# First attention block regrouped from head pairs to token tiles, with a 128-token first FFN step

## Chip, cores and metric

The kernel runs on one core of one Trainium2 chip. The metric is device time in microseconds (us): the median of 3 runs of the kernel before is 591.53 us (591.43 to 591.8).

## What is computed

Chunked attention with memory tokens, then a two-matrix feed-forward network (FFN) with a clipped quadratic gate. All inputs and outputs are float32.

```python
B, H, S, D = 4, 8, 768, 64            # 24 chunks of 32 queries in each sequence
for c in range(S // 32):
    q_c = q[:, :, 32*c : 32*c + 32]
    k_full = concat(mem_k, k[:, :, max(0, 32*c - 16) : min(S, 32*c + 32 + 8)])   # 8 + 56 keys
    v_full = concat(mem_v, v[ same rows ])
    out[:, :, chunk] = softmax(q_c @ k_full.T / sqrt(D)) @ v_full
x = out as (3072 tokens, 512)
h = x @ w_in                           # 512 x 2048
g = where(h >= 1, h, where(h <= -1, 0, (h + 1)**2 / 4))
y = g @ w_out                          # 2048 x 512
```

## The kernel before

The 3072 tokens are six blocks of 512 (TB). A block's FFN has 16 steps `fc`, one for each 128 rows of the hidden layer. A step's *hidden* part is 12 matmuls into one PSUM tile `ps_h` (x and w are each split into a high and a low float32r part, and three of the four products are kept, over four slices of the model dimension); ScalarE (ACT) then takes Relu and Square of it, VectorE (DVE) the minimum with the linear branch (*least*), ACT rounds that to `gh`, DVE forms the rest `gl`; the step's *out* part multiplies them by a slice of w_out into one accumulator bank for each 128 tokens (banks of tags `a0`, for tokens 0 to 255 of the block, and `a1`, for the others).

Weights come as 16 packed slices w_0 to w_15, which ACT and DVE must decode before use: a Prelu on ACT, a shift and an or on DVE, a copy that makes the high part on ACT, a subtraction that makes the low part on DVE (`decode`, L160). The first two slices are loaded and decoded in halves, called u0 to u3 here: u0 and u1 are the w_in slices of fc 0 and 1, u2 that of fc 2, u3 the w_out slice of fc 0.

Block 0's attention is done in four groups g0 to g3 (`first_attention`, L238). Before the change a group is 256 tokens and two of the four pairs of heads: g0 and g1 cover tokens 0 to 255, g2 and g3 tokens 256 to 511. Each goes through: scores (PE), maximum and subtraction (DVE), exponential (ACT), sum, reciprocal and multiplication (DVE), four 128x128 transposes (PE), two copies of them into `pt` (ACT), values (PE), a copy that makes the high part `xth` of x (ACT), a subtraction that makes `xtl` (DVE). g0 does its maximum and subtraction in two halves (`HALVED`, L58); g2 takes its exponential and sum in 8 ACT instructions with an accumulator (`SUMMED`, L57). FFN steps of 256 tokens, A (tokens 0 to 255) and B (256 to 511) for fc 0 to 3, follow (`early_step`, L572); J are steps of all 512 tokens. A0 needs g0 and g1; B0 needs g2 and g3.

What the engines do up to the middle of block 1 is one list written by hand or by a planner, `FIRST` (L33): each word advances one chain by one stage, and each engine runs its instructions in the order in which they come out. So an instruction that waits holds up all later ones of its engine. In the list g0 to g3 are the groups, u0 to u3 and w2 to w15 the decodes, A, B, J (and C, D, E for block 1) the FFN steps, n0 to n3 attention of later halves of blocks, and L0 to L39 the loads, in the order of a table (L646): L0 and L1 are the two parts of g0's queries and keys, L2 and L3 those of g1, L8 and L9 of g2, L12 and L13 of g3; L4, L7, L14, L15 the values of g0 to g3; L5, L6, L10, L11 the packed halves u0 to u3; L16 to L29 the slices w2 to w15; L30 the queries and keys of n0. All are issued by SyncE (SP), in order.

`PLACES` (L233) names for each group the pair of PSUM banks of its scores and of its values. From block 2 on the order comes from a regular loop over steps, which the change does not touch.

Of the kernel before, what the change touches and what calls it, by code (L numbers as in the profile page):

```python
# [30 lines left out]


FIRST = """  # L33
    L2 L0 L1 g0 g0 g0 L3 g1 g0 g0 g1 g0 g0 g1 L8 g0 L6 L5 g0 u0 g1 L10 g0 g0 g1 L9 g1 g1 u1 g2 L4 g1
    g1 u1 u0 u0 u2 g0 g2 g0 L12 u0 u0 g2 u2 u1 L13 g3 g2 g1 g0 u1 L7 g2 u2 g2 g0 g3 L11 L16 L14 g3
    L15 L30 g1 u2 g1 L17 g1 g2 g3 L19 A0 g2 A0 g3 g3 g3 u1 u3 g3 A1 A0 L18 g3 w2 g2 g3 u2 g3 u3 u3
    L25 L23 L20 L31 g2 g3 A0 A2 g2 w2 u3 g3 A1 w2 n0 A2 A1 B0 A1 w2 L29 L22 w3 B0 A1 A0 u3 L21 w2 B0
    w3 B0 w5 w3 L28 A2 L27 L26 L24 w3 L32 A0 A1 A3 w5 B1 A3 B0 w5 A3 A2 w3 A2 n0 w5 w4 B1 B1 w4 B0
    B1 B2 A2 B2 B1 B3 B1 B2 J4 B3 n0 n0 w4 w4 B2 A3 n0 w6 B3 w4 A3 B2 n0 J5 w5 A3 B2 B3 w9 J4 w6 J4  # L39
    n0 w6 w9 J4 J6 w6 J4 B3 J5 n0 J5 w7 B3 n0 w6 J7 J5 J4 w7 J6 n0 w8 w7 w7 J5 w7 w8 J6 n0 J5 w8 J8  # L40
    w11 J6 J7 J6 J7 w10 w9 n0 w8 J8 n0 n0 w12 w9 J7 J8 w8 w9 J8 J6 n0 n0 w11 w10 n0 J7 n0 w10 w10
    J10 w11 J9 J9 w11 w13 w10 J8 w12 J9 J10 n1 n1 w11 J7 n1 w12 J10 J9 J12 w12 n1 J10 w12 n1 w14 J10
    n1 J9 w14 n1 w14 J8 J11 J9 J12 w13 J12 n1 w14 J11 J12 J13 J11 C0 w15 J12 J13 J11 w13 n1 n1 n1
    L34 L33 n2 J10 J11 n1 w13 C0 C0 w14 n1 J13 n1 C1 n2 C1 n2 n2 n2 C1 w15 C0 C1 J11 w13 J14 n2 J12
    w15 n2 C1 n2 C0 J13 J14 n1 J14 J14 L36 C2 J13 n1 C2 n1 C2 n2 J15 n2 J13 n1 n2 C3 w15 J14 L35 w15
    C2 J15 J14 n2 n2 J15 J15 C2 n2 n2 C3 D0 C3 J15 D1 D0 n2 n2 D1 C3 J15 n3 D0 J15 D1 n2 C3 n2 D2
    J15 n2 J15 D3 C0 C1 D3 D0 D2 n2 D3 n2 D0 D2 n3 n2 E5 D1 D3 n2 D2 E4 C2 n2 D3 D2 D1 E4 J15 E5 E4
    C3 n3 n3 E4 E6 E5 n3 n3 n3 E4 n3 D0 D1 E8 n3 D2 E5 D3 E6 E5 E6 E6 n3 E8 E4 E7 E6 n3 E8 E8 E7 E8
    n3 E5 E6 E7 E9 E10 L38 L37 E9 E7 E7 E9 E10 E10 n3 E7 E9 E9 n3 E13 E8 n3 E10 E12 E9 E10 E10 E12
    n3 E13 E12 n3 E13 E13 E13 E12 E11 E14 E11 E12 n3 n3 E11 n3 E14 E11 n3 E11 E15 E15 E14 E15 L39  # L50
    E11 n3 E12 E14 E14 n3 E15 n3 E15 E13
"""
# [784 lines left out]
```

## Time and profile before

| | |
|---|---|
| median of 3 runs | 591.53 us |
| the profiled execution's own time | 591.96 us |
| its span | 590.1 us |
| PE (matmul) busy | 574.4 us, 97% |
| PEld (weight load) busy | 474.8 us, 80% |
| DVE busy | 332.2 us, 56% |
| ACT busy | 267.7 us, 45% |
| chain that ended last, by engine | PE 85%, DVE 6%, ACT 5%, DMA 1% |

Times in the trace are microseconds from the start of the span. Busy shares are means over stages with different limits, so the stages have to be read one by one. A row of the timeline gives start, duration, engine, line (all are L72, the helper that records every instruction), operation, output <- input, count, and in brackets the idle time before it and what ended it. Rows that merge several instructions give their joint duration; matmuls overlap, so the distance from one start to the next is the pace.

### The profile page before, as it was taken

How to read it: one execution, taken by the hardware profiler on the slowest of the kernel's cores; microseconds unless marked ns; L12 is line 12 of the kernel's file. 1: busy time of each engine (PE TensorE's matmuls, PEld its weight loads, DVE VectorE, ACT ScalarE, POOL GpSimd, SP SyncE). 2: the span in 40 equal slices, each digit the busy share in tenths (PEclk: the TensorE clock that was granted, in tenths of full speed). 3: DMA queues.
4: the chain of work that ended last, by engine and by line, in shares of the span. 5: the costliest groups of instructions: out<-in, count | busy, mean ns of one | idle time of the engine just before them, and what ended most of it. 6: DMA issues, size and time to landing. Idle time of an engine off the chain costs nothing.

```text
span 590.1 us, 12043 instructions
## 1 busy us (share of the span) xinstructions
PE 574.4 (97%) x5364; PEld 474.8 (80%) x5364; DVE 332.2 (56%) x489; ACT 267.7 (45%) x468; POOL 2.4 (0%) x7
## 2 busy tenths in 40 slices
...
GB/s 323 423 419 422 170 147 51 99 67 57 195 0 73 2 0 179 34 41 109 72 1 73 108 72 109 73 1 60 120 72 3 1 1 0 72 0 2 0 1 71
DMA packets 10709, 54.91 MB, mean 93 GB/s; under 512 B 1185, under 2 KB 1185, under 8 KB 6305
## 3 DMA queue, kind: packets, MB, share of 16 engines
...
q8 instruction: 42, 0.69, 0.5%
...
## 4 chain that ended last, share of the span: by engine, by line
PE 85%; DVE 6%; ACT 5%; DMA 1%; issue 1%; SPq 0%; DVEq 0%; ACTq 0%
PE ps_o L72 41%; PE ps_h L72 40%; PE ps_x L72 2%; PE ps_s L72 2%; ACT pr L72 2%; DMA w<-in_first_w_dram 1%; DVE pt L72 1%; DVE f L72 1%; ACT gw L72 1%; ACT f L72 1%; DVE mx L72 1%; DVE gw L72 1%; DVE gl L72 1%; DVE wr L72 1%; ACT w L72 1%
## 5 line engine op out<-in xcount | busy, mean ns | idle before, releaser
L72 PE MATMUL ps_h<-xth,wr 128*128 128x512 f32 (+1 forms) x832 | 195.4, 376 | 1.2 <-ACT pt L72 0.6
L72 PE MATMUL ps_o<-wr,gh 128*128 128x512 f32 x768 | 194.5, 390 | 0.0
L72 PEld LDWEIGHTS ps_h<-xth,wr 128*128 128x128 f32 x832 | 147.5, 188 | 31.6 <-DVE wr L72 0.9
L72 PEld LDWEIGHTS ps_o<-wr,gh 128*128 128x128 f32 x768 | 143.5, 188 | 29.6
L72 DVE SCALAR_TENSOR_TENSOR gw<-ps_h,gw 128x512 f32<-128x512 f32 (+1 forms) x104 | 67.4, 648 | 141.1 <-ACT gw L72 140.4
L72 ACT ACTIVATE gw<-ps_h 128x512 f32<-128x512 f32 (+1 forms) x104 | 58.6, 564 | 178.1 <-PE ps_h L72 173.1
L72 PE MATMUL ps_o<-wr,gl 128*128 128x512 f32 x384 | 106.9, 389 | 0.0
L72 PE MATMUL ps_h<-xtl,wr 128*128 128x512 f32 (+1 forms) x416 | 104.5, 373 | 0.0
L72 DVE TENSOR_TENSOR gl<-gw,gh 128x512 fp32r<-128x512 f32 (+1 forms) x104 | 66.8, 647 | 54.4 <-ACT gh L72 53.8
L72 ACT CAST gh<-gw 128x512 fp32r<-128x512 f32 (+1 forms) x104 | 60.6, 587 | 65.6 <-DVE gw L72 55.6
L72 PEld LDWEIGHTS ps_h<-xtl,wr 128*128 128x128 f32 x416 | 75.0, 188 | 13.9
L72 PEld LDWEIGHTS ps_o<-wr,gl 128*128 128x128 f32 x384 | 72.1, 188 | 15.0
L72 ACT ACTIVATE gw<-gw 128x512 f32<-128x512 f32 (+1 forms) x104 | 62.3, 599 | 3.3
L72 DVE STREAM_TRANSPOSE pt<-pr 32x512 f32<-32x512 f32 (+1 forms) x60 | 41.4, 699 | 1.2
L72 DVE STREAM_TRANSPOSE xt<-xr 32x512 f32<-32x512 f32 (+1 forms) x48 | 33.1, 700 | 6.6 <-ACT xr L72 6.0
L72 ACT ACTIVATE pr<-pr 128x1024 f32<-128x1024 f32 (+1 forms) x12 | 11.4, 952 | 33.2 <-DVE pr L72 33.2
...
L72 DVE COPY ob<-ps_o 128x512 f32<-128x512 f32 (+1 forms) x16 | 9.6, 622 | 23.4 <-PE ps_o L72 23.3
L72 DVE SCALAR_TENSOR_TENSOR f<-w,f 128x1024 uint32<-128x1024 uint32 (+1 forms) x18 | 19.5, 1090 | 3.6 <-ACT f L72 3.4
L72 DVE TENSOR_TENSOR wr<-f,wr 128x1024 fp32r<-128x1024 f32 (+1 forms) x18 | 19.5, 1095 | 1.0 <-ACT wr L72 1.0
L72 ACT CAST wr<-f 128x1024 fp32r<-128x1024 f32 (+1 forms) x18 | 17.0, 951 | 5.9 <-DVE f L72 5.8
...
## 6 DMA issues: line engine op xcount, KB each, us to landing
...
qk<-in_first_qk_dram SPq DMA_DIRECT2D x8, 336.0 KB, 5.9
w<-in_first_w_dram SPq DMA_DIRECT2D x4, 512.0 KB, 8.5
v<-in_first_v_dram SPq DMA_DIRECT2D x4, 512.0 KB, 10.2
```

What stands on the lines that cost most here:

```text
L72: return self.tc.keep_in_program_order(getattr(self.engine, name)(*args, **kwargs))
```

## The change

The groups g0 to g3 become tiles of 128 tokens with all four pairs of heads; g0 is tokens 0 to 127, and so on. The count and size of a group's instructions stay (32 score matmuls, a 512-column softmax, 4 transposes, 16 value matmuls, 512 columns of x); the packed queries, keys and values are laid out anew on the host, with the same bytes in each transfer. One memset of the mask falls away: tile g0 alone holds the first chunk of the sequence. The step A0 is replaced by P0 (tokens 0 to 127) and Q0 (128 to 255), each with 12 hidden matmuls of 128 columns in place of A0's 12 of 256, its own two ACT and DVE passes over 128 columns and 3 out matmuls; they share A0's gate tiles and accumulator banks. P0 needs g0 alone, Q0 g1 alone. A1 to A3 and B0 to B3 stay. The scores go to bank pair s (g1: a0), all values to a1. `FIRST` is another list from beginning to end, the loads included.

```diff
 FIRST = """
-    L2 L0 L1 g0 g0 g0 L3 g1 g0 g0 g1 g0 g0 g1 L8 g0 L6 L5 g0 u0 g1 L10 g0 g0 g1 L9 g1 g1 u1 g2 L4 g1
-    g1 u1 u0 u0 u2 g0 g2 g0 L12 u0 u0 g2 u2 u1 L13 g3 g2 g1 g0 u1 L7 g2 u2 g2 g0 g3 L11 L16 L14 g3
-    L15 L30 g1 u2 g1 L17 g1 g2 g3 L19 A0 g2 A0 g3 g3 g3 u1 u3 g3 A1 A0 L18 g3 w2 g2 g3 u2 g3 u3 u3
-    L25 L23 L20 L31 g2 g3 A0 A2 g2 w2 u3 g3 A1 w2 n0 A2 A1 B0 A1 w2 L29 L22 w3 B0 A1 A0 u3 L21 w2 B0
...
+    L0 L1 L2 L3 g0 g0 g0 L6 u1 g0 g0 g1 g0 L5 L8 L4 L9 L10 g1 g1 g1 g0 g0 u0 u0 g1 g0 g0 u0 g1 g0 g1
+    g2 g1 u1 g1 L13 L12 g2 g0 u0 g0 L11 L7 u2 u0 g2 u2 g3 u1 u2 g0 g2 g0 P0 L16 L14 g1 g1 g3 L30 g2
+    u1 g3 g2 P0 u3 g2 L15 g1 g3 u2 P0 u1 u3 u3 u2 g1 P0 g3 g2 g3 A1 w2 A1 u3 g2 g2 Q0 Q0 g3 w2 g3 A1
+    g3 g3 L19 L17 L18 u3 g2 n0 w2 Q0 P0 A1 g3 Q0 A1 n0 A2 g3 w2 Q0 A2 g3 w2 A2 n0 B0 Q0 P0 L20 L21
+    A3 B0 w3 A2 n0 L23 B0 A3 B1 w4 A1 w3 A3 w3 A2 w4 B1 B1 B0 w3 L25 L31 L29 L22 L27 B2 L26 L24 L28
...
-    PLACES = (("s", "s"), ("a0", "a0"), ("a1", "a1"), ("a1", "s"))
+    PLACES = (("s", "a1"), ("a0", "a1"), ("s", "a1"), ("s", "a1"))
...
-        for r in range(2):
-            for c in range(NCH // 2):
-                t, j = divmod(c, P // CHUNK)
+        for r in range(NP):
+            for j in range(P // CHUNK):
                 for h in range(2):
...
-        hi, lo = (x[:, 2 * u : 2 * u + 2, half * HT : (half + 1) * HT] for x in x_of(0))
+        ps = ps.rearrange("p r (t q) -> p r t q", t=2)
+        hi, lo = (x[:, :, g * P : (g + 1) * P].rearrange("p (r t) q -> p r t q", t=2) for x in x_of(0))
...
-            pair, n = divmod(len(halves), 2)
+            name = f"{blk}{tokens[0] // 2}{fc}"
+            if name not in halves:
+                halves.append(name)
+            pair, n = divmod(halves.index(name), 2)
             key = ("g", pair)
-            halves.append(name)
...
-        tiles = both[key]
-        g, gh, gl = (x[:, n * HT : n * HT + size] for x in tiles)
+        tiles, c0 = both[key], n * HT + (tokens[0] % 2) * P
+        g, gh, gl = (x[:, c0 : c0 + size] for x in tiles)
...
+    parts |= {"P": (0, (0,)), "Q": (0, (1,))}
...
-    k0 = kw[: 2 * (NCH // 2)].reshape(2, NCH // 4, 2, NP, 2, W, D)
+    k0 = kw[: 2 * (NCH // 2)].reshape(NT, 2, 2, NP, 2, W, D)
...
-    v0 = vw[0].reshape(2, 2, 4, NP // 2, 2, 2, W, D).copy()
+    v0 = vw[0].reshape(NT, 4, NP // 2, 2, 2, W, D).copy()
```

With the new list the first instructions of the engines are, in their order (a group's stages by the names used above):

```
PE:  g0 scores, g1 scores, g0 transposes, g2 scores, g1 transposes, g0 values, g3 scores, P0 hidden,
     g1 values, g2 transposes, A1 hidden, g2 values, Q0 hidden, g3 transposes, n0 scores, g3 values,
     A2 hidden, B0 hidden, Q0 out, P0 out, A3 hidden, ...
ACT: u1 Prelu, g0 exp, g1 exp, u0 Prelu, g0 pt, u0 high, u2 Prelu, g2 exps, g0 xth, g1 pt, u1 high,
     P0 Relu and Square, u3 Prelu, g1 xth, g3 exp, u2 high, P0 gh, g2 pt, w2 Prelu, A1 Relu and Square,
     u3 high, g2 xth, Q0 Relu and Square, g3 pt, ...
DVE: g0 max and subtraction (two halves), g1 max, g1 subtraction, g0 sum, u0 shift, g1 sum,
     g0 reciprocal, g0 multiplication, u0 or, g1 reciprocal, g1 multiplication, u1 shift, g2 max, ...
```

Before, they are:

```
PE:  g0 scores, g1 scores, g0 transposes, g2 scores, g1 transposes, g0 values, g3 scores, g1 values,
     g2 transposes, A0 hidden, A1 hidden, g3 transposes, g2 values, g3 values, A2 hidden, n0 scores,
     B0 hidden, A0 out, A1 out, A3 hidden, ...
ACT: g0 exp, u0 Prelu, g1 exp, u1 Prelu, u2 Prelu, g0 pt, u0 high, g2 exps, g1 pt, g0 xth, u1 high,
     u2 high, g1 xth, g3 exp, g2 pt, A0 Relu and Square, u3 Prelu, w2 Prelu, g3 pt, ...
```

## Rows read from the trace of the kernel before

**Rows 1.** The page's first part: span, then busy time, share of the span and number of instructions of each engine.

```profile
span 590.1 us, 12043 instructions
PE 574.4 (97%) x5364; PEld 474.8 (80%) x5364; DVE 332.2 (56%) x489; ACT 267.7 (45%) x468; POOL 2.4 (0%) x7
```

**Rows 2.** Busy time by stage of the span; columns: stage and its length, busy time of PE, PEld, DVE, ACT, POOL (with instructions), granted clock, DMA share, GB/s.

```profile
4.70:12.40 7.70, 2.53 (x128) 1.82 (x129) 4.68 (x12) 1.80 (x4) 0.00 (x0) 1.00 1.01 367
12.40:21.60 9.20, 7.49 (x203) 6.07 (x204) 7.88 (x18) 7.88 (x27) 0.00 (x0) 1.00 1.03 420
21.60:31.00 9.40, 8.42 (x128) 7.28 (x134) 8.20 (x16) 8.09 (x16) 0.00 (x0) 1.00 1.02 425
...
36.00:76.00 40.00, 40.00 (x318) 33.70 (x317) 37.59 (x53) 32.87 (x50) 0.00 (x0) 1.00 0.74 306
76.00:135.00 59.00, 58.43 (x771) 49.12 (x770) 46.19 (x66) 40.79 (x90) 0.00 (x0) 1.00 0.25 91
```

**Rows 3.** Who PE waited for from 40 us to the end: total, times, longest, in us.

```profile
PE ps_h L72 <- DVE gw L72: 0.4, 1, 0.4
PE ps_x L72 <- ACT pr L72: 0.2, 1, 0.2
```

**Rows 4.** Timeline of PE, 4 to 36 us.

```profile
4.68 0.68 PE L72 MATMUL ps_s<-qk 64*32 64x64 f32 x32 [1.61 <-DMA qk<-in_first_qk_dram]
6.56 1.18 PE L72 MATMUL ps_s<-qk 64*32 64x64 f32 x64 [1.19 <-DMA qk<-in_first_qk_dram]
7.89 0.68 PE L72 MATMUL ps_s<-qk 64*32 64x64 f32 x32 [0.15 <-DMA qk<-in_first_qk_dram]
12.41 1.08 PE L72 MATMUL ps_h<-ident,pr 128*128 128x128 f32 x4 [3.84 <-DVE pr L72]
...
21.25 0.66 PE L72 MATMUL ps_h<-ident,pr 128*128 128x128 f32 x4
21.66 0.48 PE L72 MATMUL ps_h<-xth,wr 128*128 128x256 f32 x2
...
28.12 1.15 PE L72 MATMUL ps_x<-pt,v 128*64 128x64 f32 x32 [0.18 <-ACT pt L72]
29.20 1.22 PE L72 MATMUL ps_h<-xth,wr 128*128 128x256 f32 x8
...
30.83 1.48 PE L72 MATMUL ps_s<-qk 64*32 64x64 f32 x128
32.24 1.22 PE L72 MATMUL ps_h<-xth,wr 128*128 128x256 f32 x8
...
33.78 1.09 PE L72 MATMUL ps_o<-wr,gh 128*128 128x512 f32 x4
...
36.53 1.12 PE L72 MATMUL ps_h<-xth,wr 128*128 128x256 f32 x8
...
37.96 1.23 PE L72 MATMUL ps_h<-xth,wr 128*128 128x256 f32 x8
```

**Rows 5.** SP's issues (start, duration; the first five are L2, L0, L1, L3, L8, the next three L6, L5, L10), and then, from one short window for each, the time from issue to landing (last number, us) of L2, L8, L6 and L5.

```profile
0.73 2.27 SPq L72 DMA_DIRECT2D qk<-in_first_qk_dram  x5
3.05 1.60 SPq L72 DMA_DIRECT2D w<-in_first_w_dram  x3
...
qk<-in_first_qk_dram SPq DMA_DIRECT2D x1, 336.0 KB, 3.1
...
qk<-in_first_qk_dram SPq DMA_DIRECT2D x1, 336.0 KB, 6.1
w<-in_first_w_dram SPq DMA_DIRECT2D x1, 512.0 KB, 6.9
w<-in_first_w_dram SPq DMA_DIRECT2D x1, 512.0 KB, 7.7
```

**Rows 6.** Timeline of DVE: g0's mask, g0's last subtraction, g0's multiplication by the reciprocal.

```profile
7.38 0.11 DVE L72 MEMSET ps_s<- 32x64 f32 x1 [6.26 <-PE ps_s L72]
...
8.78 0.42 DVE L72 TENSOR_TENSOR pr<-ps_s,mx 128x256 f32<-128x256 f32 x1
...
11.58 0.69 DVE L72 TENSOR_TENSOR pr<-pr,rin 128x512 f32<-128x512 f32 x1
```

**Rows 7.** ACT: the stretch from g0's copy of `pt` to the end of g3's (length, busy time), then from its timeline the first of g2's exponentials, g1's `pt`, g0's `xth`, two high parts, Relu and Square of A0, two Prelus (u3, and w2 of twice the width), g3's `pt`.

```profile
13.85:28.07 14.22, 12.55 (x35) 1.00 1.02 423
...
16.59 0.31 ACT L72 ACTIVATE pr<-ps_s,mx 128x64 f32<-128x64 f32 x1 [0.25 <-DVE mx L72]
...
18.92 1.19 ACT L72 COPY pt<-ps_h 64x512 f32<-64x512 f32 x2
20.14 0.59 ACT L72 CAST xth<-ps_x 128x512 fp32r<-128x512 f32 x1
20.62 1.14 ACT L72 CAST wr<-f 128x512 fp32r<-128x512 f32 x2
...
24.53 0.38 ACT L72 ACTIVATE gw<-ps_h 128x256 f32<-128x256 f32 x1
24.95 0.42 ACT L72 ACTIVATE gw<-gw 128x256 f32<-128x256 f32 x1
25.27 1.73 ACT L72 ACTIVATE w<-w 128x512 f32<-128x512 f32 x2
26.90 1.17 ACT L72 COPY pt<-ps_h 64x512 f32<-64x512 f32 x2
```

More of the change, by code (lines that the diff above doesn't have):

```diff
@@ L33 @@
 FIRST = """
-    L2 L0 L1 g0 g0 g0 L3 g1 g0 g0 g1 g0 g0 g1 L8 g0 L6 L5 g0 u0 g1 L10 g0 g0 g1 L9 g1 g1 u1 g2 L4 g1
-    g1 u1 u0 u0 u2 g0 g2 g0 L12 u0 u0 g2 u2 u1 L13 g3 g2 g1 g0 u1 L7 g2 u2 g2 g0 g3 L11 L16 L14 g3
-    L15 L30 g1 u2 g1 L17 g1 g2 g3 L19 A0 g2 A0 g3 g3 g3 u1 u3 g3 A1 A0 L18 g3 w2 g2 g3 u2 g3 u3 u3
-    L25 L23 L20 L31 g2 g3 A0 A2 g2 w2 u3 g3 A1 w2 n0 A2 A1 B0 A1 w2 L29 L22 w3 B0 A1 A0 u3 L21 w2 B0
-    w3 B0 w5 w3 L28 A2 L27 L26 L24 w3 L32 A0 A1 A3 w5 B1 A3 B0 w5 A3 A2 w3 A2 n0 w5 w4 B1 B1 w4 B0
@@ L39 @@
[L39 to L48, printed above, removed]
@@ L49 @@
-    n3 E5 E6 E7 E9 E10 L38 L37 E9 E7 E7 E9 E10 E10 n3 E7 E9 E9 n3 E13 E8 n3 E10 E12 E9 E10 E10 E12
-    n3 E13 E12 n3 E13 E13 E13 E12 E11 E14 E11 E12 n3 n3 E11 n3 E14 E11 n3 E11 E15 E15 E14 E15 L39
-    E11 n3 E12 E14 E14 n3 E15 n3 E15 E13
+    L0 L1 L2 L3 g0 g0 g0 L6 u1 g0 g0 g1 g0 L5 L8 L4 L9 L10 g1 g1 g1 g0 g0 u0 u0 g1 g0 g0 u0 g1 g0 g1
+    g2 g1 u1 g1 L13 L12 g2 g0 u0 g0 L11 L7 u2 u0 g2 u2 g3 u1 u2 g0 g2 g0 P0 L16 L14 g1 g1 g3 L30 g2
+    u1 g3 g2 P0 u3 g2 L15 g1 g3 u2 P0 u1 u3 u3 u2 g1 P0 g3 g2 g3 A1 w2 A1 u3 g2 g2 Q0 Q0 g3 w2 g3 A1
@@ new lines @@
+    g3 g3 L19 L17 L18 u3 g2 n0 w2 Q0 P0 A1 g3 Q0 A1 n0 A2 g3 w2 Q0 A2 g3 w2 A2 n0 B0 Q0 P0 L20 L21
+    A3 B0 w3 A2 n0 L23 B0 A3 B1 w4 A1 w3 A3 w3 A2 w4 B1 B1 B0 w3 L25 L31 L29 L22 L27 B2 L26 L24 L28
+    B1 B3 w4 B0 w3 L32 A3 B2 B0 B1 B2 w5 w5 B2 w4 B3 A3 n0 B3 w5 w6 w9 n0 w4 w7 w6 w6 B2 A2 J4 n0 B3
+    w6 J4 n0 B1 J4 w5 B3 w5 J5 w9 J4 J5 B2 A3 n0 B3 n0 J6 n0 w6 w7 J5 J4 w7 n0 n0 J5 J4 J7 n0 J5 n0
+    w8 J6 w7 J7 J6 w11 J6 n0 w7 J7 w9 n0 w8 J6 w10 w14 J8 w8 J5 n0 w8 J8 w9 w8 J8 J8 J8 w9 w10 n1 n1
@@ new lines @@
+    J9 w10 w12 w13 J7 J9 w12 n1 J7 J9 n1 w12 J6 L33 L34 J7 J9 w10 C0 w12 n1 n1 n1 J8 w10 C0 C0 n1 C1
+    J10 w11 n1 w12 J9 w11 w15 C0 C1 w11 w14 C1 n1 n1 w11 n1 J9 C1 J10 C1 n1 J11 n2 w13 C0 J10 w13
+    J11 J11 J10 w13 J11 J13 n1 J10 n2 J13 n2 J10 n2 n2 J12 n2 w14 w14 n2 J11 n2 n1 J11 J12 w13 J13
+    n1 w15 J12 n1 J12 w15 J12 J14 C2 n2 J13 n2 J12 n2 J14 J13 n1 J14 L35 w14 J13 C3 C2 w15 C2 J15 n2
+    w15 n2 C3 J14 n2 n2 C3 J14 n2 C2 J15 J14 D0 n2 L36 J15 n2 J15 J15 D1 C3 n3 D1 n2 D1 J15 n2 J15
@@ L52 @@
+    n2 J15 D0 D0 D0 D1 C0 D2 C2 n2 n2 C3 J15 D2 J15 D0 E5 D1 E5 D2 C1 E4 D0 n2 n3 E5 D1 D2 D3 E5 D3
+    E5 D3 D3 C2 E4 n2 C3 E6 E4 D3 E4 D2 E4 D2 n3 D3 E9 E9 n3 E6 E9 n3 E6 E4 E9 E6 E7 E8 E6 E7 E9 E8
+    E8 E7 E5 n3 n3 E7 E7 E6 E10 n3 L37 E7 n3 E11 n3 E10 E8 n3 E8 E11 E8 E10 E11 n3 E10 E12 E13 n3
+    E10 E11 E12 E12 E14 n3 n3 E9 E10 E12 E12 E11 n3 E13 E13 E14 E11 n3 E15 E12 E13 E13 E14 n3 E15 n3
+    n3 E15 E14 E13 n3 n3 E15 E15 L39 L38 n3 n3 E14
 """
@@ L239, in first_attention @@
         half, u = divmod(g, 2)
-        c0 = half * NCH // 2
-        src = qk_of[0, g].rearrange("p (r n) -> p r n", r=2)
+        src = qk_of[0, g].rearrange("p (r n) -> p r n", r=NP)
         ps = two_banks(PLACES[g][0], "ps_s")[:, :, 0:HT]
-        s = ps.rearrange("p h (r t w) -> p h r t w", r=2, w=W)
-        for r in range(2):
-            for c in range(NCH // 2):
-                t, j = divmod(c, P // CHUNK)
+        s = ps.rearrange("p h (r w) -> p h r w", w=W)
+        for r in range(NP):
+            for j in range(P // CHUNK):
                 for h in range(2):
-                    rows, k0 = slice(h * D, (h + 1) * D), HT + c // 2 * PAIR + c % 2 * (PAIR - W)
+                    rows, k0 = slice(h * D, (h + 1) * D), P + j // 2 * PAIR + j % 2 * (PAIR - W)
                     pe.matmul(
-                        s[j * CHUNK : (j + 1) * CHUNK, h, r, t],
-                        src[rows, r, c * CHUNK : (c + 1) * CHUNK],
+                        s[j * CHUNK : (j + 1) * CHUNK, h, r],
+                        src[rows, r, j * CHUNK : (j + 1) * CHUNK],
                         src[rows, r, k0 : k0 + W],
@@ L256, in first_attention @@
         yield
-        for c in range(NCH // 2):
-            t, j = divmod(c, P // CHUNK)
-            mask(c0 + c, s[j * CHUNK : (j + 1) * CHUNK, :, :, t], c % 2 * NM)
+        for j in range(P // CHUNK):
+            mask(g * P // CHUNK + j, s[j * CHUNK : (j + 1) * CHUNK], j % 2 * NM)
         if u == 0:
@@ L606, in early_step @@
             acc.setdefault(blk, [None] * NT)
-            pair = two_banks(f"a{tokens[0] // 2}", "ps_o")
-            for t in tokens:
-                acc[blk][t] = pair[:, t % 2]
+            if acc[blk][tokens[0]] is None:
+                pair, t = two_banks(f"a{tokens[0] // 2}", "ps_o"), tokens[0] // 2 * 2
+                acc[blk][t : t + 2] = pair[:, 0], pair[:, 1]
         wh, wl = weights(1, fc, 0), weights(1, fc, 1)
@@ L775, in _lay_out @@
     kw = windows(mem_k, k)
-    k0 = kw[: 2 * (NCH // 2)].reshape(2, NCH // 4, 2, NP, 2, W, D)
+    k0 = kw[: 2 * (NCH // 2)].reshape(NT, 2, 2, NP, 2, W, D)
     k0 = _np.concatenate([k0[:, :, 0], k0[:, :, 1, :, :, W // 2 :], k0[:, :, 1, :, :, :NM]], axis=4)
-    k0 = k0.transpose(0, 3, 5, 2, 1, 4).reshape(2, 2 * D, NP, -1)
+    k0 = k0.transpose(0, 3, 5, 2, 1, 4).reshape(NT, 2 * D, NP, -1)
+    q0 = qt[0:2].reshape(2, 2 * D, NP, 2, 128).transpose(0, 3, 1, 2, 4).reshape(NT, 2 * D, NP, 128)
     kw = kw.reshape(NB * 2, NCH // 4, 2, NP, 2, 2, W // 2, D)
```

6 lines of the change are left out of this document (3 added, 3 removed).

## Prediction

> **What bounds the kernel now.** I read the busy shares first: PE is busy for 574.4 of 590.1 us [rows 1], and the chain of waits ends on PE, so time can be won or lost only where PE stands idle, or by more PE work. The table by stage then shows where: 5.17 us idle of the 7.70 from 4.7 us on, 1.71 in the next 9.20, 0.98 in the next 9.40, nothing from 36 to 76, 0.57 in the 59 us after that [rows 2]; from 40 us on PE waits for 0.6 us in all [rows 3]. The regular loop is untouched. So the question is when PE has done one set of work: all of g0 to g3, the scores of n0, the hidden parts of A0, A1, A2 and B0. Before, that is at 33.78 us, where the first out part starts [rows 4]; the set left is the same afterwards (P0 and Q0 with three out matmuls each stand for A0's six).
>
> What holds PE in that stretch? From 12.4 to 31 us DVE is busy for 16.1 and ACT for 16.0 of 18.6 us [rows 2], and PE's waits end on them. So the two queues are near full, and both run strictly in the listed order. I therefore walk the new lists, with start-to-start distances from the rows.
>
> **The start.** Landings in the old order, as issue plus latency or as the PE start that waited: L2 3.83, L0 4.68, L1 6.56, L3 7.89, L8 8.65, L6 9.95, L5 11.25 [rows 4, 5]. They follow the order of issue, so I take landing as a function of kilobytes ahead (336 for queries and keys, 512 for half a slice). In the new order L0 lands at 3.83, L1 at 4.68, L2 and L3 as the second and third pair did, 6.56 and 7.89; L6 is now fifth (1856 KB, between 1680 at 8.65 and 2192 at 9.95) at about 9.1, L5 (2368 KB) at 10.4. g0's scores end about 1.85 us earlier, at 5.4, and its last subtraction at 7.35 instead of 9.2 [rows 6].
>
> This gain is lost at once, in three places. On ACT u1's Prelu is listed ahead of g0's exponential and waits for L6: 9.1 to 9.75, so the exponential ends at 10.3. On DVE g1's maximum and subtraction stand ahead of g0's sum; they need L3 and end at 10.05; the sum runs from 10.35 to 11.05. Then u0's shift stands between g0's sum and its reciprocal: it needs u0's Prelu, which follows g1's exponential, 10.75 to 11.4; the shift ends at 11.85, g1's sum at 12.45, and g0's multiplication runs from 12.6 to 13.3, against 11.58 to 12.27 [rows 6]. The transposes start at 13.45 instead of 12.41 and take 1.08 [rows 4], so g0's `pt` copy starts at 14.5, not 13.85.
>
> **From there ACT sets the pace.** Prices [rows 7]: a pair of `pt` copies 1.18; `xth` 0.52 (0.48 to the next start, 0.59 by itself); a high part 0.57; g2's exponentials 2.33 (16.59 to 18.92); Relu and Square at 256 columns 0.74; a Prelu 0.58, at twice the width 1.05. Check on the old list, from g0's `pt` to g3's: 4 pt, 3 high parts, g2's exponentials, 2 xth, g3's exponential (0.57), A0, u3 and w2 make 12.7, where the row has 12.55 busy of 14.22.
>
> The new list has in the same stretch four high parts (2.28), three xth (1.56), u2's Prelu as well (0.58 more), A1 (0.74) in place of A0, and P0 and Q0. A 128-column Relu and Square is not in the trace; its bounds are half of 0.74 and 0.74. I take 0.53, as two instructions with a fixed part each, so 1.06, and 0.2 for P0's `gh`. The sum: 4.72 + 2.28 + 2.33 + 1.56 + 0.57 + 2.21 + 0.74 + 1.06 + 0.2 = 15.7 us. From 14.5 on, without a wait, g3's `pt` ends at 30.2. Waits: for P0's hidden part about 0.3 (u1's high part ends at 21.6, P0's hidden part at 21.8, after the scores of g3, which need the bank of g2's exponentials), for g2's maximum 0.15, for Q0's hidden part 0.3; I take 0.7 (bounds 0 and the old stretch's 1.67). So 30.9 instead of 28.07.
>
> Ahead of g3's values PE now also has n0's scores, which outlast the copy by 0.2 (1.41 against 1.18); their load L30 comes ahead of L15 on SP now, but at 420 GB/s [rows 2] both are in by about 27. What is left is g3's values 1.08, A2 1.43 (36.53 to 37.96) and B0 1.54 (32.24 to 33.78) [rows 4]: 30.9 + 0.25 + 1.08 + 1.43 + 1.54 = 35.2, against 33.78. **Loss: 1.4 us.**
>
> **The narrow hidden parts.** P0 and Q0 have 24 matmuls of 128 columns where A0 had 12 of 256, at 0.119 us each (1.43 for 12). No float32r matmul of 128 columns is in the trace. From below: half of it, 0.06. The nearest row is the four transposes, also 128 columns against 128x128 weights of 4-byte values: 21.25 to 21.66, 0.103 each. From above: full float32 values, 32 instructions of 64 columns in 1.15 (28.12), 0.072 for each matmul's pair of instructions, 0.144 at twice the columns, and 0.29 if the two heads run side by side. I take 0.119, that is 1.43 for each of P0 and Q0, and the walk has it in it. In the middle of the upper bounds, 0.216, each would be 1.16 longer; P0 and Q0 both stand ahead of ACT instructions that wait for them, so 2.3 us come on top.
>
> On this the Trainium skill speaks too: "TensorE: Matmul & The Clock Gate", section "Back-to-back issue gap", gives some 81 ns a matmul at 128 columns in a sustained stream. The transposes' 103 ns disagree upwards, though they are few; by 81 ns the two parts would be 0.9 shorter in all and the loss about 0.5. Its section "LDWEIGHTS (loading the stationary operand)" has the load of 128 columns at 128/1.2 = 107 ns whatever the rows, which would be the limit at 128 columns; the 103 ns bear that out better, and the loss by it is 1.1.
>
> **Other edits.** One memset less: 0.11 on DVE, before g1's maximum, which waits for L3 anyway. P0's and Q0's extra DVE passes (4 for 2) add some 0.3 us while DVE is 94% busy, 36 to 76 us [rows 2]; PE is then 1.4 later, so its deadlines are too, and this costs nothing; were the cover gone, 0.3. The placement in a1 orders the values behind the previous group's `xtl`, which is earlier on ACT's path already. SP has w5 ahead of w3, so w3 lands 2.5 us later; by its place in the list its low part is due at 44.7 (A2's out part) and ready at about 43.9, so nothing, at worst 1. The later list I could only compare by the same deadlines; the 0.57 us idle after 76 us may go or double.
>
> **Rivals.**
> *Narrow matmuls at 0.216 us.* For it: plain float32 is slow at 64 columns. Against it: the transposes. 1.4 + 2.3 = 3.7 us slower, 595.2. Chance 0.24.
> *The late start is made up.* If `g0` ends its multiplication by 12.3 (landings a microsecond earlier, which needs the gap of 1.88 us between the landings of L0 and L1 [rows 4], where 0.85 is usual, not to come again) the 1.0 goes, and 0.4 is left or nothing. 591.6. For it: the gap may belong to the old pattern; against it: u1's Prelu and u0's shift still stand in the way. Chance 0.17.
> *Faster: P0 and Q0 fill PE's gaps.* PE's idle 2.69 us from 12.4 to 31 closes, less 1.43 of extra PE work: 1.3 us faster, 590.2. Place: PE's queue at P0, which is ready after one group. It decides where g3's `pt` ends before 28: ACT's 15.7 us must then start by 12.3, with g0's multiplication done at 11. For it: g0's scores are 1.85 us earlier; against it: rows 5 for L6 and L5. Chance 0.10.
>
> **How the numbers follow.** The forecast has the chance 0.49. The profiled execution took 591.96, 0.43 over the median; I add the loss to the median: 591.53 + 1.4 = 592.9. Its own range, from no waits on ACT to the 1.67 of old and 0.3 on DVE, is 591.9 to 594.2. Changes under 0.2% (1.18 us) can't be told from none in this kernel. Of the forecast's 0.49, 0.21 lies under that bound; with the late start made up that is 0.38 for no change. Slower: 0.28 + 0.24 = 0.52. Faster: 0.10. The range leaves out half of the faster and a good third of the narrow case: 590.7 to 595.5.
>
> **What would show it.** In the profile after: g0's exponential on ACT behind a Prelu that waited for the load, ending near 10.3; g0's transposes at 13.4; g3's `pt` ending near 31; the first out part on PE at about 35.2; P0's 12 matmuls in 1.4 us (2.6 says the rival). The forecast is wrong if the transposes start before 12.5, if the first out part comes before 34, or if PE has more than 1 us of idle after 36.

## The result and the profile after

The changed kernel took 596.52 us (median of 4, 595.03 to 596.89) against 591.66 us, a ratio of 1.0077 with a 95% interval of 1.0062 to 1.0092: slower by 4.9 us where 1.4 were forecast, and above the range. Five more executions of the same kernel in a later study took 594.13 us (593.56 to 594.42), 1.0043 (1.0030 to 1.0055). Both belong to the answer (the second lies inside the range), and the profiles of one of each show why they differ.

The page of the first profile, its first part, beside [rows 1]:

```profile
span 595.1 us, 12067 instructions
PE 578.7 (97%) x5376; PEld 478.5 (80%) x5376; DVE 332.6 (56%) x490; ACT 267.7 (45%) x471; POOL 2.4 (0%) x7
```

The added work is small: 12 matmuls, 1 instruction on DVE, 3 on ACT. PE's busy time has grown by 4.3 us, though, three times what 12 matmuls at 0.119 us make. By stage (columns as in [rows 2]):

```profile
12.40:21.60 9.20, 7.14 (x172) 5.99 (x173) 7.52 (x19) 6.86 (x24) 0.00 (x0) 1.00 1.04 422
21.60:31.00 9.40, 8.39 (x97) 7.70 (x96) 6.91 (x15) 6.68 (x15) 0.00 (x0) 1.00 1.01 417
...
76.00:135.00 59.00, 58.02 (x762) 48.47 (x762) 47.73 (x66) 43.09 (x91) 0.00 (x0) 1.00 0.20 73
```

From 21.6 to 31 us PE is as busy as before (8.39 against 8.42), but with 97 matmuls instead of 128, and ACT and DVE are busy for 6.7 and 6.9 us instead of 8.1 and 8.2. That suggests that PE is slow and that they wait for it; the timelines show it. PE's timeline, answering to [rows 4]:

```profile
13.47 1.09 PE L72 MATMUL ps_h<-ident,pr 128*128 128x128 f32 x4 [4.86 <-DVE pr L72]
...
16.64 1.98 PE L72 MATMUL ps_x<-pt,v 128*64 128x64 f32 x32
19.61 1.19 PE L72 MATMUL ps_s<-qk 64*32 64x64 f32 x64 [0.99 <-ACT pr L72]
20.72 1.97 PE L72 MATMUL ps_h<-xth,wr 128*128 128x128 f32 x8
22.49 1.05 PE L72 MATMUL ps_h<-xtl,wr 128*128 128x128 f32 x4
23.48 1.98 PE L72 MATMUL ps_x<-pt,v 128*64 128x64 f32 x32
...
29.18 1.15 PE L72 MATMUL ps_x<-pt,v 128*64 128x64 f32 x32
30.26 1.11 PE L72 MATMUL ps_h<-xth,wr 128*128 128x128 f32 x8
31.21 0.61 PE L72 MATMUL ps_h<-xtl,wr 128*128 128x128 f32 x4
...
37.68 0.63 PE L72 MATMUL ps_o<-wr,gh 128*128 128x512 f32 x2
```

P0's hidden part runs from 20.72 to 23.48, 2.76 us; Q0's, the same instructions, from 30.26 to 31.66, 1.40. The 32 value matmuls take 1.98 us at 16.64 and 23.48 and 1.15 at 29.18. Narrow matmuls are not slow; PE ran at about half its pace until some 26 us. On ACT:

```profile
9.20 0.66 ACT L72 ACTIVATE w<-w 128x512 f32<-128x512 f32 x1 [7.18 <-DMA w<-in_first_w_dram]
9.75 1.14 ACT L72 ACTIVATE pr<-pr 128x512 f32<-128x512 f32 x2
...
23.58 0.28 ACT L72 ACTIVATE gw<-ps_h 128x128 f32<-128x128 f32 x1 [1.86 <-PE ps_h L72]
...
24.11 0.67 ACT L72 ACTIVATE w<-w 128x512 f32<-128x512 f32 x1
25.50 0.59 ACT L72 CAST xth<-ps_x 128x512 fp32r<-128x512 f32 x1 [0.73 <-PE ps_x L72]
...
31.86 0.28 ACT L72 ACTIVATE gw<-ps_h 128x128 f32<-128x128 f32 x1 [0.43 <-PE ps_h L72]
...
32.38 1.16 ACT L72 COPY pt<-ps_h 64x512 f32<-64x512 f32 x2
```

ACT stood 1.86 us for P0's hidden part, with g3's chain behind it in its queue, then 0.73 for g1's values (`xth`) and 0.43 for Q0's hidden part: g3's `pt` ends at 33.54, not 30.9, and the first out part starts at 37.68.

### The profile page after: what moved, and what is told of

The parts are those of the page before. It is cut to its first block, busy times and chain, and to the rows that moved or that the text cites. A ratio compares the mean times of both kernels' runs of the same rounds, so it can differ in the third digit from the quotient of the medians.

```text
span 595.1 us, 12067 instructions
## 1 busy us (share of the span) xinstructions
PE 578.7 (97%) x5376; PEld 478.5 (80%) x5376; DVE 332.6 (56%) x490; ACT 267.7 (45%) x471; POOL 2.4 (0%) x7
## 4 chain that ended last, share of the span: by engine, by line
PE 84%; DVE 3%; ACT 3%; issue 1%; DVEq 0%; ACTq 0%
PE ps_o L72 40%; PE ps_h L72 40%; PE ps_x L72 2%; PE ps_s L72 2%; DVE f L72 1%; ACT gw L72 1%; ACT pr L72 1%; DVE gl L72 1%; DVE pt L72 1%; DVE wr L72 1%; ACT wr L72 0%; ACT w L72 0%; ACT gh L72 0%; ACT xth L72 0%; DVE gw L72 0%
## 5 line engine op out<-in xcount | busy, mean ns | idle before, releaser
L72 PE MATMUL ps_h<-xth,wr 128*128 128x512 f32 (+2 forms) x840 | 196.3, 376 | 0.0
L72 PEld LDWEIGHTS ps_h<-xth,wr 128*128 128x128 f32 x840 | 149.6, 190 | 29.0 <-issue 0.2
L72 DVE SCALAR_TENSOR_TENSOR gw<-ps_h,gw 128x512 f32<-128x512 f32 (+2 forms) x105 | 67.4, 643 | 145.7 <-ACT gw L72 145.3
L72 ACT ACTIVATE gw<-ps_h 128x512 f32<-128x512 f32 (+2 forms) x105 | 58.7, 559 | 183.6 <-PE ps_h L72 179.5
L72 PE MATMUL ps_h<-xtl,wr 128*128 128x512 f32 (+2 forms) x420 | 105.6, 374 | 1.0 <-DVE xtl L72 1.0
L72 DVE TENSOR_TENSOR gl<-gw,gh 128x512 fp32r<-128x512 f32 (+2 forms) x105 | 67.3, 644 | 57.9 <-ACT gh L72 57.5
L72 ACT CAST gh<-gw 128x512 fp32r<-128x512 f32 (+2 forms) x105 | 60.5, 581 | 66.2 <-DVE gw L72 52.2
L72 ACT ACTIVATE gw<-gw 128x512 f32<-128x512 f32 (+2 forms) x105 | 62.5, 595 | 3.4
L72 ACT ACTIVATE w<-w 128x1024 f32<-128x1024 f32 (+1 forms) x18 | 18.2, 1035 | 7.2 <-DMA w<-in_first_w_dram 7.2
```

The source lines that it names most:

```text
L72: return self.tc.keep_in_program_order(getattr(self.engine, name)(*args, **kwargs))
```

## The experiments

Times are medians over five rounds; the kernel before ran on the same chip in each study (591.66 to 591.8 us). Theory 1 in the expectations is that PE's slower pace at P0 is the loss, theory 2 that narrow matmuls are slow by themselves, theory 3 that the order of the queues is.

### One group: is it PE's pace, the narrow matmuls or the queues?

**a_warm.** Ten matmuls on zeros into PE's idle time ahead of g0's transposes.

```diff
-    L0 L1 L2 L3 g0 g0 g0 L6 u1 g0 g0 g1 g0 L5
+    L0 L1 L2 L3 g0 g0 g0 L6 u1 g0 g0 g1 K10 g0 L5
...
+    def start_warm(n):
+        keep_warm(n)
+        yield
```

> The changed kernel with ten 512-column bf16 matmuls on zeros put between g1's scores and g0's transposes, into PE's idle time there (8.6 to 13.5 us); nothing of the result depends on them. Theory 1 (PE runs at half pace from 13.5 to 26 us because it had stood idle): P0's 12 hidden matmuls take about 1.45 us instead of 2.76, g1's values 1.15 instead of 1.98, g3's pt copy ends at about 31 instead of 33.5, first out part at about 35.3 instead of 37.7, and the time falls by about 2.3 us. Theory 2 (128-column float32r matmuls are slow there by themselves): P0 stays at 2.7 us and the time within 0.7 us. Theory 3 (only the order of the queues counts, a late start that ACT carries on): no change either, or worse by what the ten matmuls delay the transposes.

596.8 us: no gain. Its PE timeline:

```profile
8.62 4.45 PE L72 MATMUL ps_h<-warm 128*128 128x512 bf16 x10
13.53 0.63 PE L72 MATMUL ps_h<-ident,pr 128*128 128x128 f32 x4 [0.47 <-DVE pr L72]
...
15.89 1.15 PE L72 MATMUL ps_x<-pt,v 128*64 128x64 f32 x32
19.41 0.86 PE L72 MATMUL ps_s<-qk 64*32 64x64 f32 x64 [2.37 <-ACT pr L72]
20.20 1.94 PE L72 MATMUL ps_h<-xth,wr 128*128 128x128 f32 x8
...
38.08 0.50 PE L72 MATMUL ps_o<-wr,gh 128*128 128x512 f32 x1 [0.58 <-issue]
```

After the ten matmuls the pace is up: transposes 0.63 us instead of 1.09, values 1.15. But after the next idle time of 2.4 us, g3's scores still take 0.86 us and P0 then runs at half pace again. Here the granted clock tells it (columns: stage, length, PE busy, granted clock, DMA share, GB/s):

```profile
22.00:24.00 2.00, 2.00 (x25) 0.50 1.00 422
```

So theory 1's remedy failed before it reached P0, and the run decides nothing on its price.

**b_warm.** Eight such matmuls in the kernel before.

```diff
-    L2 L0 L1 g0 g0 g0 L3 g1 g0
+    L2 L0 L1 g0 g0 g0 L3 g1 K8 g0
```

> The kernel before with eight such matmuls between g1's scores and g0's transposes (idle 8.6 to 12.4 us). Theory 1: g0's and g1's transposes (1.1 us each), g2's scores (1.4) and g0's values (1.85) run at full pace, together about 2 us of PE work less, but ACT sets the pace there, so the time falls by 0 to 0.6 us. Theory 3: no change.

591.59 us, ratio 0.9996 (0.9987 to 1.0004).

```profile
20.08 1.98 PE L72 MATMUL ps_x<-pt,v 128*64 128x64 f32 x32
...
33.78 1.09 PE L72 MATMUL ps_o<-wr,gh 128*128 128x512 f32 x4
```

On ACT, first in this run and then, just behind the same place, in the profiled execution of before:

```profile
22.11 0.59 ACT L72 CAST xth<-ps_x 128x512 fp32r<-128x512 f32 x1 [0.43 <-PE ps_x L72]
```

```profile
22.80 0.63 ACT L72 ACTIVATE pr<-pr 128x512 f32<-128x512 f32 x1 [0.56 <-DVE pr L72]
```

Eight such matmuls did not raise the pace: the transposes after them take 1.08 us, and at 20 us PE is at half pace (g1's values 1.98; in the profiled execution of before they took 1.15, at 20.16). And yet the first out part starts at 33.78, as before. ACT waits 0.43 us for the slow values, but in before it waits 0.56 for DVE just behind that place; g3's exponential starts at 22.72 against 22.80. So the kernel before, in these two profiles, does not feel PE's pace up to 22 us: no FFN part stands that early in ACT's queue, and the slower values fall into a wait that is there anyhow.

**a_warm2.** a_warm, and seven more into the free bank pair a0 ahead of g3's scores.

```diff
-    L11 L7 u2 u0 g2 u2 g3 u1
+    L11 L7 u2 u0 g2 H7 u2 g3 u1
...
+    def hold_warm(n):
+        ps = two_banks("a0", "ps_k")[:, 0]
+        for _ in range(n):
+            pe.matmul(ps, warm[:, 0:P], warm, start=True, stop=True)
+        yield
```

> The changed kernel with ten idle matmuls on zeros ahead of g0's transposes and seven more (into the free bank pair a0) ahead of g3's scores, where PE waits for g2's exponentials. In a_warm PE ran at full pace from 13.5 us, but the gap of 2.4 us before g3's scores was followed by half pace again. Theory 1 (PE's pace at P0 is the loss): full pace from 13.5 us on, P0's 12 matmuls in 1.45 us, first out part at about 35.2 us and the time 2 to 2.5 us under the changed kernel's 596.5. Theory 2 (narrow matmuls are slow by themselves, or the pace is not set by the idle time before): P0 still 2.7 us. Theory 3 (queue order alone): P0 faster, but the first out part stays near 37.

595.68 us (594.76 to 598.13). The profiled execution is the slowest of the six:

```profile
17.33 1.68 PE L72 MATMUL ps_k<-warm 128*128 128x512 bf16 x7
...
20.69 1.11 PE L72 MATMUL ps_h<-xth,wr 128*128 128x128 f32 x8
21.64 0.61 PE L72 MATMUL ps_h<-xtl,wr 128*128 128x128 f32 x4
...
36.82 0.50 PE L72 MATMUL ps_h<-xth,wr 128*128 128x256 f32 x2 [1.83 <-issue]
```

Now P0 takes 1.49 us to the next start (20.69 to 22.18): theory 2 falls. The first out part starts at 37.63, though, near 37 as theory 3 has it. Between the two lies a stop of 1.83 us at which PE waits for nothing that the profile knows. Without it the first out part would start at 35.8, where theory 1 has 35.2 and the transposes start 0.6 later than in the changed kernel (14.04 against 13.47). In this execution the granted clock then falls as well, to its lower level for part of two stretches, and 8 matmuls of 256 columns take 1.91 us at 39.63 instead of 1.12:

```profile
38.00:40.00 2.00, 2.00 (x8) 0.57 0.99 414
40.00:42.00 2.00, 2.00 (x13) 0.57 1.06 430
```

(columns: stage, length, PE busy, granted clock, DMA share, GB/s). The other five executions, at 594.8 to 596.5, are no faster than the changed kernel in a_again; they have no profile.

**a_again.** The changed kernel, unaltered.

> The changed kernel once more, for its scatter. Theory 1 (PE's pace at P0 is a matter of when the chip raises it, and P0 stands in ACT's queue, so the time shows it): the times fall into two groups about 2 us apart, near 595 and near 596.8, while those of the kernel before stay together; if the profiled execution is one of the lower group, its P0 takes about 1.45 us and its first out part starts at about 35.3. Rival (one slow pace always, the scatter is something else): P0 takes 2.7 us whatever the time.

594.13 us, and the profiled execution (594.42) is a fast-paced one:

```profile
13.71 1.09 PE L72 MATMUL ps_h<-ident,pr 128*128 128x128 f32 x4 [4.83 <-DVE pr L72]
...
20.64 1.11 PE L72 MATMUL ps_h<-xth,wr 128*128 128x128 f32 x8
...
22.13 1.15 PE L72 MATMUL ps_x<-pt,v 128*64 128x64 f32 x32
...
35.49 0.63 PE L72 MATMUL ps_o<-wr,gh 128*128 128x512 f32 x2
```

```profile
22.23 0.28 ACT L72 ACTIVATE gw<-ps_h 128x128 f32<-128x128 f32 x1 [0.27 <-PE ps_h L72]
...
29.67 0.28 ACT L72 ACTIVATE gw<-ps_h 128x128 f32<-128x128 f32 x1 [0.42 <-PE ps_h L72]
...
30.20 1.16 ACT L72 COPY pt<-ps_h 64x512 f32<-64x512 f32 x2
```

One kernel, two paces: P0 takes 1.49 us (20.64 to 22.13) or 2.76, ACT's wait is 0.27 or 1.86, g3's `pt` ends at 31.36 or 33.54, the first out part starts at 35.49 or 37.68, the span is 592.6 or 595.1. This settles the larger part: 2.2 of the 3.5 us by which the forecast was short are PE's pace at P0 and g1's values. The five new times did not fall into two groups, as expected, but all into the lower one; taken with the first four, this kernel's nine times lie at 593.56 to 595.03 (six) or 596.24 to 596.89 (three). Both groups turn up within one study on one chip in a_start and a_tail below, so it isn't a matter of the chip alone.

### The start, the step, the later list

**a_start.** u1's Prelu behind g0's exponential, u0's Prelu and shift behind g0's multiplication.

```diff
-    L0 L1 L2 L3 g0 g0 g0 L6 u1 g0 g0 g1 g0 L5 L8 L4 L9 L10 g1 g1 g1 g0 g0 u0 u0 g1 g0 g0 u0 g1 g0 g1
+    L0 L1 L2 L3 g0 g0 g0 L6 g0 g0 g1 g0 u1 L5 L8 L4 L9 L10 g1 g1 g1 g0 g0 g1 g0 g0 u0 u0 u0 g1 g0 g1
```

> The changed kernel with the start of the list alone reordered: u1's Prelu behind g0's exponential on ACT, u0's Prelu and shift behind g0's multiplication. All theories: g0's transposes at about 12.3 us instead of 13.47. Theory 3: the 1.1 us are carried on by ACT to the first out part, and the time falls by about 1 us. Theory 1: less, if PE is still slow until 26 us: P0's hidden part stays at 2.7 us, and the time falls by 0.5 to 1 us.

594.94 us, from 593.24 to 596.97: three executions at 593.2 to 594.1, three at 595.8 to 597.0, so its median says little. The profiled one, of the faster three, has P0 at full pace:

```profile
12.61 1.08 PE L72 MATMUL ps_h<-ident,pr 128*128 128x128 f32 x4 [3.89 <-DVE pr L72]
...
34.88 0.63 PE L72 MATMUL ps_o<-wr,gh 128*128 128x512 f32 x2
```

The transposes come 1.10 earlier than in a_again, the first out part only 0.61; the start is carried on, but not whole. The faster executions of the two kernels differ by less (593.2 to 594.1 against 593.6 to 594.4).

**a_A0.** A0 in Q0's place in the list, P0's words dropped.

```diff
-    g3 g3 L19 L17 L18 u3 g2 n0 w2 Q0 P0 A1 g3 Q0 A1 n0 A2 g3 w2 Q0 A2 g3 w2 A2 n0 B0 Q0 P0 L20 L21
+    g3 g3 L19 L17 L18 u3 g2 n0 w2 A0 A1 g3 A0 A1 n0 A2 g3 w2 A0 A2 g3 w2 A2 n0 B0 A0 L20 L21
```

> The changed kernel with A0 (256 tokens) in Q0's place and no P0: what the 128-token step itself costs. Theory 1: P0's 2.76 us at half pace and ACT's wait of 1.86 us for it go, so g3's pt copy ends near 31.3 and the time falls by about 2 us. Theory 3: P0 and Q0 fill time that PE had idle, the time stays within 0.5 us or rises.

595.85 us, neither theory's number: 0.7 under the first median, 1.7 over a_again's. The scatter is small (595.52 to 595.96), as it should be if the time no longer shows PE's pace without P0. g3's `pt` ends at 31.02, as expected (31.3), but the first out part starts at 36.65, later than a_again's, because PE stops in n0's scores:

```profile
29.45 1.04 PE L72 MATMUL ps_s<-qk 64*32 64x64 f32 x80
31.95 0.71 PE L72 MATMUL ps_s<-qk 64*32 64x64 f32 x48 [1.47 <-issue]
```

**a_regroup.** a_A0 with a_start's start.

```diff
-    L0 L1 L2 L3 g0 g0 g0 L6 u1 g0 g0 g1 g0 L5 L8 L4 L9 L10 g1 g1 g1 g0 g0 u0 u0 g1 g0 g0 u0 g1 g0 g1
+    L0 L1 L2 L3 g0 g0 g0 L6 g0 g0 g1 g0 u1 L5 L8 L4 L9 L10 g1 g1 g1 g0 g0 g1 g0 g0 u0 u0 u0 g1 g0 g1
...
-    u1 g3 g2 P0 u3 g2 L15 g1 g3 u2 P0 u1 u3 u3 u2 g1 P0 g3 g2 g3 A1 w2 A1 u3 g2 g2 Q0 Q0 g3 w2 g3 A1
+    u1 g3 g2 u3 g2 L15 g1 g3 u2 u1 u3 u3 u2 g1 g3 g2 g3 A1 w2 A1 u3 g2 g2 A0 A0 g3 w2 g3 A1
```

> The changed kernel with the start of a_start and with A0 in place of P0 and Q0: the regrouping, its loads and the rest of its list alone. In a_A0 PE stood for 1.5 us in n0's scores, at its 476th matmul, without a releaser in the profile. Theory 3 (late start and queue order): g0's transposes near 12.4, g3's pt copy ending near 30.2, first out part near 34.4 and the time 592.3 to 593.0, unless PE stands still at the same matmul again. Rival (PE's instruction stream holds it up): a stop without a releaser at matmul 476 or 603, some 6 us after the 349th or 476th, the first out part again after 35 us and the time at 594 or more. Either way little scatter, since no FFN part stands early in ACT's queue.

594.76 us (594.1 to 595.12). Transposes at 12.19 and g3's `pt` to 30.20, as theory 3 has them, then the stop at the same matmul, as the rival has it, and the first out part at 35.55; less the stop it would start at 34.37 (34.4 expected). PE was at half pace until some 22 us here (g1's values 1.88 at 19.90), and the small scatter stays:

```profile
28.63 1.04 PE L72 MATMUL ps_s<-qk 64*32 64x64 f32 x80
30.85 0.71 PE L72 MATMUL ps_s<-qk 64*32 64x64 f32 x48 [1.18 <-issue]
```

**b_PQ.** The kernel before with P0 and Q0 side by side at each of A0's words (`early_step` as changed).

```diff
-    L15 L30 g1 u2 g1 L17 g1 g2 g3 L19 A0 g2 A0 g3 g3 g3 u1 u3 g3 A1 A0 L18 g3 w2 g2 g3 u2 g3 u3 u3
+    L15 L30 g1 u2 g1 L17 g1 g2 g3 L19 P0 Q0 g2 P0 Q0 g3 g3 g3 u1 u3 g3 A1 P0 Q0 L18 g3 w2 g2 g3 u2 g3 u3 u3
...
+    parts |= {"P": (0, (0,)), "Q": (0, (1,))}
```

> The kernel before with P0 and Q0, one after the other, at each of A0's places; grouping and list else as before. What the narrow parts cost by themselves. Theory 1: 24 matmuls at 0.119 us for 12 at 0.119 where PE is already at full pace, 1.4 us less what falls into idle time (0.6 us at 24 us), so the time rises by 0.8 to 1.5 us. Theory 2 (0.22 us a matmul whatever the pace): it rises by 3 us or more.

593.4 us, ratio 1.0037 (1.0024 to 1.0050): 1.7 us slower, a little over the expected 0.8 to 1.5, with a short stop of 0.32 in it.

```profile
22.51 1.21 PE L72 MATMUL ps_h<-xth,wr 128*128 128x128 f32 x8
23.56 0.61 PE L72 MATMUL ps_h<-xtl,wr 128*128 128x128 f32 x4
24.24 1.11 PE L72 MATMUL ps_h<-xth,wr 128*128 128x128 f32 x8
...
38.03 0.39 PE L72 MATMUL ps_o<-wr,gl 128*128 128x512 f32 x1 [0.32 <-issue]
```

A narrow hidden part costs as much as a wide one here, 1.7 us to the next start and 1.4: the second one is all extra. Theory 2's 3 us are out.

**a_tail.** The changed list up to J6's first word, then the remaining words in the order of before.

```diff
-    w5 B3 w5 J5 w9 J4 J5 B2 A3 n0 B3 n0 J6 n0 w6 w7 J5 J4 w7 n0 n0 J5 J4 J7 n0 J5 n0 w8 J6 w7 J7 J6 w11
+    w5 B3 w5 J5 w9 J4 J5 B2 A3 n0 B3 n0 J6 J4 J5 w6 J7 J5 J4 w7 J6 w8 w7 w7 J5 w7 w8 J6 n0 J5 w8 J8 w11
...
```

> The changed kernel up to J6's first word, then the remaining words in the order of the kernel before. In the changed kernel the first out part is 3.9 us late but the end 4.95 us. Theory A (the later list loses the other 1.05 us, half of it idle PE time at 85 and 111 us): the time falls by about 1 us to 595.5, and PE's idle time from 76 to 135 us falls to 0.5 us or less. Rival B (the 1.05 us are lost for another reason, since both lists keep PE busy): the time stays at 596.5.

594.38 us: four executions at 593.9 to 594.7, two at 596.3 and 596.4 (the first of these is the profiled one; P0 takes 2.75 us in it).

**a_tail_again.** The same once more.

> The changed kernel with the later list of before, once more. Its times were 593.9 to 594.7 and 596.3, and the profile was one of the latter, with P0 at 2.75 us. Theory 1: an execution of the lower group has P0 at about 1.45 us and its first out part near 35.2 us; lower and upper group stand 2.0 to 2.4 apart. Rival: the same pace in both, and another difference.

594.64 us, all five in the lower group; the profiled one, at full pace, has its first out part at 35.34 and a span of 592.4, against 35.49 and 592.6 in a_again. The order of the later list is not the loss: theory A falls. PE's idle time after 76 us is back at 0.57, but 0.34 stand before 76 instead, and from the first out part to the end it still loses 0.66 us (last matmul at 587.50, 2.22 after before's 585.28, less 1.56). In the changed list that loss is 0.77 (a_again) to 1.05 (first profile), of which 0.42 is more PE idle time from 76 to 135 us; the rest stays open.

**a_all.** a_start's start, idle matmuls in both gaps (8 and 7) and a_tail's list.

```diff
-    L0 L1 L2 L3 g0 g0 g0 L6 u1 g0 g0 g1 g0 L5
+    L0 L1 L2 L3 g0 g0 g0 L6 g0 g0 g1 K8 g0 u1 L5
...
-    L11 L7 u2 u0 g2 u2 g3 u1
+    L11 L7 u2 u0 g2 H7 u2 g3 u1
```

> The changed kernel with all three suspected losses taken away together: the start of a_start, idle matmuls in both of PE's gaps (8 and 7), the later list of a_tail. If the losses add up as told (1.1 for the start, about 2.4 for PE's pace, 1.0 for the later list), the first out part is at about 34.7 us and the time at 592.0 to 592.6, steady from run to run (a_start alone scattered from 593.2 to 597.0). If one of them is not the cause, the time stays above 593.5.

594.97 us (594.0 to 595.63), steadier than a_start, but not 592.0 to 592.6: the losses do not simply add up. PE is at full pace and P0 takes 1.49, and then:

```profile
32.80 1.12 PE L72 MATMUL ps_h<-xth,wr 128*128 128x256 f32 x8
35.51 0.74 PE L72 MATMUL ps_h<-xtl,wr 128*128 128x256 f32 x4 [1.59 <-DVE gw L72]
```

The releaser named, A2's *least* on DVE, had ended at 34.7 and is no input of these matmuls; g3's `xtl`, which is, had ended at 33.3. So this is taken for a stop like the others. Less the 1.59 the first out part, at 36.09, would start at 34.5 (34.7 expected).

**b_start.** The kernel before with g0's chain pulled ahead of everything at the start, and the decodes put behind the first copies.

```diff
-    L2 L0 L1 g0 g0 g0 L3 g1 g0 g0 g1 g0 g0 g1 L8 g0 L6 L5 g0 u0 g1 L10 g0 g0 g1 L9 g1 g1 u1 g2 L4 g1
+    L0 L1 L2 L3 L8 L9 g0 g0 g0 g1 g0 g0 g0 L4 L6 L5 L7 g0 g0 g0 g0 g0 g1 g1 g1 g2 g0 g1 g1 g1 g1 g1
+    g0 L10 L12 u1 g2 g1 L13 g2 u1 u0 u0 u0 g0 g3 g1 u0 g2 g2 g2 g0 u0 u1 g1 u2 u1 u2 g3 g1 u2 L11
...
```

> The kernel before, its grouping and steps unchanged, with another start of the list: g0's and g2's queries and keys earlier in the loads, g0's sum, reciprocal and multiplication before g1's maximum, the decodes of u0 to u2 behind the first copies on ACT. If ACT's queue from g0's pt copy on sets the end of the start (theory 3 as far as the kernel before goes), g0's transposes start at about 10 us instead of 12.4, g3's pt copy ends at about 27.2 instead of 28.1, the first out part starts at about 33.0, and the time falls by 0.5 to 1 us. Rival: PE's instruction stream (matmul 603 of the program was not issued before 35.5 us in any run, some 6 us after matmul 476) holds PE up, and the time stays within 0.5 us.

597.04 us, 5.4 slower: both predictions wrong. The transposes start at 10.01, but g0's values not before 15.15 (1.98, at half pace), and u0's Prelu, put behind g2's exponentials, ends at 19.5; DVE stands 4.4 us for it, A0 waits for g1's `xtl` and A1 for g2's `pt` (2.43 us at 28.11). What was pulled ahead had nothing to feed, and the run says nothing on the stops.

### Where PE stops without a releaser

Counting matmuls in program order, a_A0 and a_regroup stop right after the 476th, and a_warm, a_warm2, a_all and b_PQ after the 603rd, though other instructions stand there: 127 matmuls apart, 254 instructions with their weight loads. Each stop ends 2.5 to 3.1 us after the start of the half microsecond in which a packet shows on the queue that the page calls "instruction". In a_regroup that is 28.0 to 28.5, in a_all 32.5 to 33.0 (columns: packets, MB, share of the 16 DMA engines):

```profile
q8 instruction: 1, 0.02, 12.7%
```

```profile
q8 instruction: 1, 0.02, 12.8%
```

and some 6 us after PE had passed the stop before (a_all: the 476th at about 29.4, released at 35.51). In the other eight profiles the 604th matmul starts some 2.9 to 4.0 us after such a packet, and PE does not stop there. The Trainium skill's "Runtime: NRT & Kernel Launch", section "Instruction fetch mechanics", says that instructions come in blocks of 16 KiB, 256 instructions, the next one fetched while one runs, and that this is mostly hidden. The spacing is close to that (254 recorded instructions); that it is hidden does not hold here, with the DMA engines 100% busy, if the block is what PE waits for. That is inferred from place and time in six kernels, not shown; no run removed it alone. The kernel before passes its 603rd matmul at about 37.7, 3 to 4 us after its packet at 34.0 to 34.5, without a stop. By this reading it could be only about 1 us earlier there; no variant had its first out part before 33.78.

## Why the prediction was wrong

*The start* held: transposes at 13.47 (forecast 13.45), g0's exponential behind u1's Prelu (9.75), u0's shift in the way, g0's `pt` at 14.65 (14.5). With that the rival of a late start made up is out: g0's multiplication ended at 13.32, not by 12.3.

*ACT's sum* held at full pace. Relu and Square of 128 columns took 0.53 us to the next start (23.58 to 24.11), P0's `gh` 0.20, both as taken; its waits for PE there were 0.69 (0.27 for P0's hidden part and 0.42 for Q0's; 0.7 was forecast for all waits); g3's `pt` ended at 31.36 in a_again (30.9, with transposes 0.26 later), the first out part started at 35.49 (35.2). This part of the loss, 1.7 us at the first out part, rests on the walk agreeing with the trace. a_start's mended start took 0.6 off it; no variant took off the rest by itself, since the stops came in between.

*The narrow hidden parts* were priced right for themselves: 0.119 us a matmul (Q0 1.40, forecast 1.43). The 81 ns of the Trainium skill, "TensorE: Matmul & The Clock Gate", section "Back-to-back issue gap", would have misled. The step that failed is the wait for P0: I took PE's pace there from rows in which it had already risen, so ACT's waits up to g3's `pt` were put at 0.7 us, 0.3 of it for P0, with 1.67 as the upper bound. In the first profile its waits for PE alone were 3.02: 1.86 for P0's hidden part, 0.73 for g1's values, 0.43 for Q0's hidden part. [rows 4] hold the warning, unread: the transposes take 1.08 us at 12.41 and 0.66 at 21.25. Idle matmuls of 512 columns fit the clock's two levels: 4.45 us for ten in a_warm (0.44 each) and 1.68 for seven in a_warm2 (0.24 each), where 512 columns make 0.43 at 1.2 GHz and 0.21 at 2.4. In a_warm the granted clock reads 0.50 while P0 runs at this pace (8 matmuls in 1.94 us, 1.97 in the first profile), so the slower pace is the clock's lower level, 1.2 GHz. In the profiles of before and after the same column reads 1.00 in the slow stretches at the start, so there it didn't tell. At half pace P0 and g1's values take 1.3 and 0.8 us more, and ACT waits for both.

*The first rival* gave 595.2, nearest to the 596.5, by luck: about its 0.216 us a matmul was measured (0.22, 1.77 for eight), but by PE's pace and not by width. Its price left out g1's values and g2's transposes, which the same pace lengthens, and took Q0 for slow too.

*The stretch behind the first out part*, taken as nothing, costs 0.8 to 1.05 us. With the 2.2 of the pace and 0.3 at the first out part this makes the 3.5 us that were missing. a_tail_again, with the later words in the order of before, still loses 0.66, so it isn't their order alone. PE's longer idle time from 76 to 135 us is 0.42 of it; 0.3 to 0.6 us are unexplained.

*The faster rival* needed g3's `pt` to end before 28; even a_regroup, with the start mended and no P0, had 30.20.
